# Twelve scalings by a third, made by GpSimd instead of VectorE, in a gated dilated convolution

## The chip, the core and the metric

The kernel runs on one core of a Trainium2 chip. A core has TensorE (matrix products, "PE" in the profile), VectorE ("DVE"), ScalarE ("ACT"), GpSimd ("POOL") and SyncE ("SP", which issues transfers here), each with its own queue of instructions, worked off in order. SBUF is the on-chip memory; PSUM holds what TensorE sums up. The metric is the device time of one execution in microseconds (us).

## The reference

The input x has 2 sequences of 16000 steps with 256 channels, in bf16. A causal convolution with three taps, two steps apart, makes 512 channels; the first 256 go through tanh, the others through a sigmoid; their product is multiplied by a 256x256 matrix.

```python
dil = 2
pad = (K - 1) * dil                      # K = 3
h = xp[t + 4] @ w[0] + xp[t + 2] @ w[1] + xp[t] @ w[2]   # xp: x with pad zeros ahead
f, g = h[..., :256], h[..., 256:]
z = tanh(f) * sigmoid(g)
out = z @ w_o
```

## The kernel before, in words

**Groups.** The time axis is cut into groups. One short group (kind P) at the start is computed tap by tap. The others save matrix products by the algebra of fast convolutions. A group of kind B takes four neighbouring steps a row, two pairs of outputs, and needs four products instead of six. A group of kind A takes six steps a row, three pairs of outputs, and needs five products instead of nine. There are 13 A groups (numbered 0 to 12) of 256 rows. What the products multiply are not the inputs but sums of them, each a tile of 128 partitions by 1024 bf16 elements (two steps of the pair, two halves of the channels, 256 rows). For an A group `operand` (L325) names them:

- u0, u1, u2, e: differences, and f: a sum, of two views of the input tile xt;
- u3 = u1 / 3, uh = -u1 / 2, ud = 2 u1: the scalings;
- rm = e + u3, rp = f + u1, r0 = u0 + uh, ri = u2 + ud: these replace e, f, u0 and u2 in place (`ON_TOP`, L362), and TensorE multiplies them. It also multiplies u1 itself. So in the profile TensorE reads them under the names e, f and u.

**Who makes them.** `pre` (L365) issues one of these operations on the engine that it is given, for all four quarters of 256 elements or for a slice of them. VectorE makes the differences and the scalings. GpSimd makes ri, quarter by quarter, and part of the operands m, p, d0 and d3 of the B groups. rm, rp and r0 are made by transfers that add while they land (L377), issued from GpSimd's queue. So u3 has one reader: the transfer that adds it onto e. The tiles of u3 rotate through two buffers (`sum_pool`), those of e, f and u through three.

**After the products.** TensorE sums the products into PSUM banks. ScalarE copies the first one to SBUF (ss, L432). VectorE combines (L435): a, and for A groups also hh and yy, each 128x512 fp32 from one SBUF and one PSUM operand. ScalarE applies tanh and sigmoid (L475), VectorE multiplies the two (the gate, zz, L494, two SBUF operands in bf16), TensorE multiplies by w_o (L512), ScalarE moves the result to SBUF (L537) and SyncE stores it.

**What sets the order.** The order of all queues is written out by hand in `PLAN` (L13), one line for each of the blocks, with four fields: TensorE, ScalarE, VectorE, GpSimd. A block is one group and one of four tiles of 128 output channels. Tokens of the third field are VectorE's instructions in order: a, y, h (the combinations), g (a gate product), v, and names such as `u3.4`, which means u3 of A group 4. Tokens of the fourth field are GpSimd's, and are issued where the third field has its `a`. A token of the fourth field that computes is held (`hold`, L353): it waits for the VectorE instruction that was issued last, or one before it for every apostrophe (`made_v`, `gpsimd`, L569). The call gives the reason: "GpSimd reads SBUF while VectorE's sums read PSUM". Such a line is

```python
 F Z P L I | a y c b e e | g u0.4 u3.4 f.4 a y | r0.3 ri.3 m.6''
```

Here VectorE makes a gate product, u0, u3 and f of group 4, then a and y; GpSimd issues the transfer r0 of group 3, a quarter of ri of group 3 and a quarter of m of B group 6.

The loop over the lines dispatches the tokens of the third field one by one; what is none of the letters goes to `sums` (L565), which calls `pre` with VectorE and notes the instruction for later holds.

Of the kernel before, what the change touches and what calls it, by code (L numbers as in the profile page):

```python
# [123 lines left out]
def kernel(  # L124
# [10 lines left out]
    nc = tc.nc  # L135
# [189 lines left out]
    def operand(g, name):  # L325

        G = groups[g]
        R = G["R"]
        prev, cur = views(g)
        v = lambda n: G[n][:, :, :, :R]  # L330
        if G["kind"] == "B":
            return {
                "m": lambda: (ALU.subtract, None, cur[0], prev[1]),
                "p": lambda: (ALU.add, None, cur[0], prev[1]),
                "d0": lambda: (ALU.subtract, None, prev[0], cur[0]),
                "d3": lambda: (ALU.subtract, None, cur[1], prev[1]),
            }[name]()
        return {
            "u0": lambda: (ALU.subtract, None, prev[1], cur[0]),
            "u1": lambda: (ALU.subtract, None, prev[2], cur[1]),  # L340
            "u2": lambda: (ALU.subtract, None, cur[2], cur[0]),
            "e": lambda: (ALU.subtract, None, cur[0], prev[2]),
            "f": lambda: (ALU.add, None, cur[0], prev[2]),
            "rp": lambda: (ALU.add, None, v("f"), v("u1")),
            "u3": lambda: (None, 1.0 / 3.0, v("u1"), None),
            "rm": lambda: (ALU.add, None, v("e"), v("u3")),
            "uh": lambda: (None, -0.5, v("u1"), None),
            "ud": lambda: (None, 2.0, v("u1"), None),
            "r0": lambda: (ALU.add, None, v("u0"), v("uh")),
            "ri": lambda: (ALU.add, None, v("u2"), v("ud")),  # L350
        }[name]()

    def hold(ins, behind):  # L353
        if behind is not None:
            tc.add_manual_dep(
                ins.ins, behind.ins.name,
                mybir.DependencyInfo(mybir.DependencyClass.Sync, mybir.DependencyReason.DATA),
                reason="GpSimd reads SBUF while VectorE's sums read PSUM",
            )
        return ins  # L360
# [4 lines left out]
    def pre(g, name, eng, qs=slice(0, 4), behind=None):  # L365
        G = groups[g]
        R = G["R"]
        op, factor, a, b = operand(g, name)
        if name not in G:
            if name in ON_TOP:  # L370

                G[name] = G[ON_TOP[name]]
            else:
                pool = {"m": pre_pool, "p": pre_pool, "u3": sum_pool, "uh": sum_pool, "ud": sum_pool, "d0": dif_pool, "d3": dif_pool}.get(name, dif_pool)
                G[name] = pool.tile([P, 2, CT, RG], bf16, name=name, tag=name)
        if name in BY_DMA:
            return nc.gpsimd.dma_start(out=G[name][:, :, :, :R], in_=b, accum_op=op)  # L377
        o, a, b = (t if t is None else t.rearrange("p q ct r -> p (q ct) r")[:, qs] for t in (G[name][:, :, :, :R], a, b))
        if op is None:
            ins = eng.tensor_scalar_mul(o, a, factor)  # L380
        else:
            ins = eng.tensor_tensor(out=o, in0=a, in1=b, op=op)  # L382
        return hold(ins, behind)
# [43 lines left out]
    def copy_first(blk):  # L427
        g, oi = blk
        G = groups[g]
        n = 2 * G["R"]  # L430
        G["ss", oi] = ss_pool.tile([P, 2 * RG], f32, name="ss")
        nc.scalar.copy(out=G["ss", oi][:, :n], in_=G["b", oi][:, :n])  # L432
# [84 lines left out]
    def out_evict(g, rb0, jp, on_v=False):  # L517
        G = groups[g]
        J = G["J"]
        o_ps = G["o", rb0, jp]  # L520
        copy = (lambda **a: note(nc.vector.tensor_copy(**a))) if on_v else nc.scalar.copy  # L521
        t0 = G["t0"] + J * rb0
        if jp is None:
            odd = osb_pool.tile([P, D], bf16, name="odd", tag="odd")
            copy(out=odd[:], in_=o_ps[:, 0, :])
            n = G["R"] - rb0
            assert J * n == P
            store = dict(out=out[G["b"], t0:t0 + J * n, :].rearrange("(r q) d -> q r d", q=J), in_=odd[:])
            if g == seq[-1][0]:
                last_odd.append(store)  # L530
            else:
                nc.sync.dma_start(**store)
            return
        if ("osb", rb0) not in G:
            G["osb", rb0] = osb_pool.tile([P, J, D], bf16, name="osb", tag=f"osb{J}")
        osb = G["osb", rb0]
        copy(out=osb[:, 2 * jp:2 * jp + 2, :], in_=o_ps[:])  # L537
        G["out", rb0] = G.get(("out", rb0), 0) + 1
        if G["out", rb0] == J // 2:
            nc.sync.dma_start(  # L540
                out=out[G["b"], t0:t0 + J * P, :].rearrange("(p j) d -> p j d", j=J), in_=osb[:]
            )
# [14 lines left out]
    def note(ins):  # L557
        made_v.append(ins)
        return ins

    def group_of(token):
        name, n = token.split(".")
        return (Bs if name in ("m", "p", "d0", "d3") else As)[int(n)], name

    def sums(tokens):  # L565
        for token in tokens:
            note(pre(*group_of(token), nc.vector))
# [54 lines left out]
    for k, line in enumerate(PLAN.strip().split("\n"), -1):  # L622
        pe, act, dve, pool = (part.split() for part in line.split("|"))
        b0, b1, b2, b3 = (seq[n] if 0 <= n < N else None for n in (k, k - 1, k - 2, k - 3))
        if ">" in dve:
            sums(dve[:dve.index(">")])
            dve = dve[dve.index(">") + 1:]
        waiting, done = list(act), set()

        def scalar():  # L630

            while waiting:
                what = waiting[0]
                there = {"c": "F" in done, "b": "Z" in done, "e": made, "E": made[1:], "d": not leftover}
                if not there.get(what, True):
                    break
                waiting.pop(0)
                if what == "c":
                    copy_first(b0)
                elif what in "by":  # L640
                    activate(b2, what)
                elif what == "a":
                    activate(b3, "a")
                elif what == "d":
                    activate((0, 3), "a")
                elif what == "w":
                    weights_a(1 + K)
                else:
                    out_evict(*made.pop("eE".index(what)))

        scalar()
        for what in pe:
            if what in "FM":
                product(b0, {"F": "first", "M": "mid"}[what])
            elif what == "L":
                product(b1, "last")
            elif what in "ZI":
                product(b2, {"Z": "zero", "I": "inf"}[what])
            elif what == "D":
                direct(3, (leftover.pop(0),), (1,))  # L660
            elif what == "H":
                piece, (bank, tag) = next(firsts)
                out_mm(*piece, dts=(0,), pool=bank, tag=tag)
            elif what == "R":
                made.append(next(seconds))
                out_mm(*made[-1], dts=(1,))
            else:
                made.append(todo.pop(0))
                out_mm(*made[-1], **({"pool": ps_b, "tag": "b"} if what == "p" else {}))
            done.add(what)  # L670
            scalar()
        assert not waiting, (k, waiting)

        for what in dve:
            if what == "g":
                gate(b3[0], b3[1] // 2)
                if b3[1] == 3 and b3 != seq[-1]:
                    todo += pieces_of(b3[0])
            elif what == "G":
                gate(0, int(k > 0))  # L680
                if k > 0:
                    todo += pieces_of(0)
            elif what == "a":
                gpsimd(pool)
                combine(b1, "a")
            elif what == "y":
                combine(b1, "y")
            elif what == "h":
                halfway(b0)
            elif what == "v":  # L690
                out_evict(*made.pop(0), on_v=True)
            else:
                sums((what,))

        while loaded < len(loads) and wanted[loads[loaded]] <= k + LOAD:
            load(loads[loaded])
            loaded += 1
# [34 lines left out]
```

## Time and profile before

| what | value |
| --- | --- |
| time, two runs | 263.03 and 263.12 us, median 263.07 |
| span of the profiled execution, first to last instruction | 261.4 us |
| the profiled execution's time outside the span, by the runs' median | 1.7 us |
| granted TensorE clock | 0.999 |
| VectorE's instructions that scale a 128x1024 tile (u3, uh, ud) | 3 x 13 |

The profile is of one execution. Its lines give an engine, a line of the kernel, the operation, the tiles as out<-in with the buffer numbers left out, and the shape. In the timelines the first two columns are the start, counted from the span's start, and the duration, in us; x2 at the end means two instructions merged, and brackets give the idle time ahead and what ended it. In the groups' rows the numbers behind the bar are the busy time in us and the mean duration in ns. Because u3 is a tile of the name u with a number, it stands in the profile as u; the scaling by a third is the row "TENSOR_SCALAR u<-u" of L380. On GpSimd, "u<-u,ud" is a quarter of ri.

### The profile page before, as it was taken

The page shows a single profiled execution, that of the slowest core. Times are in us where ns is not written, and L with a number is a line of the kernel's source. Part 1 is how long each engine was busy: PE and PEld are TensorE (multiplying, and loading weights), DVE is VectorE, ACT ScalarE, POOL GpSimd, SP SyncE. Part 2 cuts the span into 40 slices and gives each one's busy share as a digit, 9 for nine tenths or more (in the row PEclk, how much of TensorE's full clock was granted, in tenths as well). Part 3 has the DMA queues.
Part 4 walks back from the last instruction along what each step waited for, and adds up shares of the span by engine and source line. Part 5 has one row for each costly group of instructions (what it writes and reads, how often), then busy time and mean ns, then how long its engine had stood idle before and what let it go on. Part 6 is the DMA issues. An engine that isn't in the chain of part 4 may idle for free.

```text
span 261.4 us, 4534 instructions
## 1 busy us (share of the span) xinstructions
PE 256.5 (98%) x1484; PEld 144.2 (55%) x1484; DVE 240.5 (92%) x401; ACT 243.7 (93%) x492; POOL 136.2 (52%) x204
## 2 busy tenths in 40 slices
PE   8999999999999999999999999999999999999993
PEld 5654565545545555555555555555555555665682
DVE  2899999999999999999999999999999999977773
ACT  4989998999999999999999999999999999999993
POOL 1033355687765577956757685643746453431100
PEclk9999999999999999999999999999999999999999
DMA  6999979999969667969895799959825574462115
GB/s 185 215 168 212 262 177 174 227 211 179 212 152 232 139 147 143 228 147 230 197 197 135 175 214 190 239 160 201 237 41 127 149 152 116 129 160 109 76 61 210
DMA packets 81663, 45.20 MB, mean 173 GB/s; under 512 B 68936, under 2 KB 70216, under 8 KB 81640
## 3 DMA queue, kind: packets, MB, share of 16 engines
q1 hardware_dynamic: 75112, 33.74, 54.6%
q0 software_dynamic: 5616, 10.23, 23.2%
q10 hardware_dynamic: 912, 0.95, 1.1%
q8 instruction: 11, 0.18, 0.3%
q14 instruction: 12, 0.10, 0.1%
HBM read 1.25 MB, written 16.38 MB: 67 GB/s over the span
## 4 chain that ended last, share of the span: by engine, by line
PE 97%; DMA 1%; DVE 0%; issue 0%
PE b L401 57%; PE o_ps L512 21%; PE a L401 16%; PE b L421 1%; PE a L421 1%; DMA xn<-in_x_dram 1%; PE tp L308 0%; DVE osb L521 0%; PE fill L248 0%
## 5 line engine op out<-in xcount | busy, mean ns | idle before, releaser
L435 DVE SCALAR_TENSOR_TENSOR a<-ss,b 128x512 f32<-128x512 f32 (+2 forms) x100 | 67.1, 672 | 7.9 <-ACT sg L475 3.1
L537 ACT CAST osb<-o_ps 128x512 bf16<-128x512 f32 x119 | 69.8, 622 | 0.8 <-PE o_ps L512 0.7
L512 PE MATMUL o_ps<-wo_sb,zz 128*128 128x256 bf16 x496 | 70.5, 273 | 0.0
L432 ACT COPY ss<-b 128x512 f32<-128x512 f32 (+2 forms) x100 | 59.6, 597 | 4.6 <-PE b L401 3.5
L512 PEld LDWEIGHTS <-zz 128*128 128x128 bf16 x496 | 48.4, 98 | 25.2 <-DVE zz L494 0.2
L401 PEld LDWEIGHTS <-w_sb 128*128 128x128 bf16 x400 | 39.0, 98 | 36.8 <-issue 0.2
L382 POOL TENSOR_TENSOR u<-u,ud 128x256 bf16<-128x256 bf16 x52 | 39.8, 772 | 24.9 <-DVE zz L494 9.1
L382 POOL TENSOR_TENSOR d<-xt 128x256 bf16<-128x256 bf16 (+2 forms) x56 | 33.4, 606 | 32.7 <-DVE zz L494 13.0
L494 DVE TENSOR_TENSOR zz<-th,sg 128x1536 bf16<-128x1536 bf16 (+2 forms) x52 | 40.9, 788 | 0.5 <-ACT sg L475 0.2
L435 DVE SCALAR_TENSOR_TENSOR yy<-hh,b 128x512 f32<-128x512 f32 x52 | 35.4, 680 | 1.9 <-PE b L401 1.8
L435 DVE SCALAR_TENSOR_TENSOR hh<-ss,b 128x512 f32<-128x512 f32 x52 | 35.4, 681 | 1.2 <-PE o_ps L512 0.5
L475 ACT ACTIVATE sg<-b 128x512 bf16<-128x512 f32 (+2 forms) x50 | 30.5, 610 | 2.1 <-PE b L401 1.4
L475 ACT ACTIVATE th<-b 128x512 bf16<-128x512 f32 (+2 forms) x50 | 30.5, 610 | 1.9 <-PE b L401 1.6
L475 ACT ACTIVATE sg<-a 128x512 bf16<-128x512 f32 (+2 forms) x50 | 31.0, 619 | 0.0
L401 PE MATMUL b<-f,wp_sb 128*128 128x512 bf16 x104 | 30.9, 379 | 0.0
L401 PE MATMUL b<-u,w_sb 128*128 128x512 bf16 x104 | 30.9, 379 | 0.0
L401 PE MATMUL a<-u,w_sb 128*128 128x512 bf16 x104 | 30.9, 379 | 0.0
L401 PE MATMUL b<-u,wa_sb 128*128 128x512 bf16 x104 | 30.9, 379 | 0.0
L401 PE MATMUL b<-e,wm_sb 128*128 128x512 bf16 x104 | 30.9, 378 | 0.0
L475 ACT ACTIVATE th<-a 128x512 bf16<-128x512 f32 (+2 forms) x50 | 30.5, 614 | 0.3 <-PE a L401 0.2
L401 PEld LDWEIGHTS <-wp_sb 128*128 128x128 bf16 x200 | 19.5, 98 | 20.1 <-issue 0.7
L401 PEld LDWEIGHTS <-wm_sb 128*128 128x128 bf16 x200 | 19.5, 98 | 17.0 <-issue 0.4
(59 smaller groups left out, 342.7 us busy)
## 6 DMA issues: line engine op xcount, KB each, us to landing
out_dram<-osb SPq DMA_DIRECT2D x26, 384.0 KB, 2.6
out_dram<-osb SPq DMA_DIRECT2D x23, 256.0 KB, 3.0
f<-u POOLq DMA_DIRECT2D x13, 256.0 KB, 3.5
e<-u POOLq DMA_DIRECT2D x13, 256.0 KB, 4.4
u<-uh POOLq DMA_DIRECT2D x13, 256.0 KB, 5.3
w_sb<-in_w_dram ACTq DMA_DIRECT2D x3, 256.0 KB, 4.1
xt<-in_x_dram SPq DMA_TRANSPOSE x25, 7.2
xn<-in_x_dram SPq DMA_DIRECT2D x1, 160.0 KB, 3.2
```

The costliest lines, as they stand in the source:

```text
L382: ins = eng.tensor_tensor(out=o, in0=a, in1=b, op=op)
L401: nc.tensor.matmul(G[bank, oi][:, :2 * R], lhsT=wmat[:, ct, osl], rhs=G[mv][:, :, ct, :R], start=which == "first" and ct == 0, stop=ct == ...
L421: nc.tensor.matmul(G[bank, oi][:, :4 * r].rearrange("p (j r) -> p j r", j=4), lhsT=w_taps[tap][:, ct, osl], rhs=xt[:, j0:j0 + 4, ct, c0 + ...
L432: nc.scalar.copy(out=G["ss", oi][:, :n], in_=G["b", oi][:, :n])
L435: return note(nc.vector.scalar_tensor_tensor(out=out, in0=in0, scalar=scalar, in1=in1, op0=ALU.mult, op1=op))
L475: nc.scalar.activation(out=G[name, dt][:, j:j + 2, :R], in_=G[bank, oi][:, :2 * R].rearrange("p (q r) -> p q r", q=2), func=(ACT.Tanh, ACT ...
L494: note(nc.vector.tensor_tensor(out=G["z"][:, dt, :, :n], in0=G["th", dt][:, :, :n], in1=G["sg", dt][:, :, :n], op=ALU.mult))
L512: nc.tensor.matmul(o_ps[:, q, :], lhsT=z, rhs=wo_sb[:, dt, :], start=dt == 0 and (q == 0 or len(dts) == NT), stop=dt == NT - 1, skip_group ...
L537: copy(out=osb[:, 2 * jp:2 * jp + 2, :], in_=o_ps[:])
```

## The change

In the loop over VectorE's tokens a case is added ahead of the last one: a token u3.n with n over 0 is issued on GpSimd, in two halves of two quarters each where n is odd, in one instruction where n is even.

```diff
             elif what == "v":
                 out_evict(*made.pop(0), on_v=True)
+            elif what.startswith("u3") and int(what[3:]):
+                n = int(what[3:]) % 2 + 1
+                for q in range(0, 4, 4 // n):
+                    pre(*group_of(what), nc.gpsimd, slice(q, q + 4 // n))
             else:
                 sums((what,))
```

`pre` is called without a VectorE instruction to be held behind, and the new instructions are not noted in `made_v`, so that an apostrophe in the fourth field counts VectorE's remaining instructions. The place in the program is the token's: on GpSimd the scaling comes after what earlier lines and tokens gave it, and ahead of the fourth field's tokens of its line where u3 stands before `a`. Twelve scalings (groups 1 to 12) become 18 instructions on GpSimd: two of 128x512 for the odd groups, one of 128x1024 for the even ones. The scaling of group 0 stays on VectorE. TensorE's, ScalarE's and SyncE's instructions stay as they are.

## The prediction

> **What bounds the kernel now.** I read the engine shares first, then the chain that ended last, then TensorE's waits, then five stretches of 40 us through the steady part (their sum is quoted), and last the timelines of VectorE (DVE) and GpSimd (POOL) side by side.
>
> ```profile
> span 261.4 us, 4534 instructions
> PE 256.5 (98%) x1484; PEld 144.2 (55%) x1484; DVE 240.5 (92%) x401; ACT 243.7 (93%) x492; POOL 136.2 (52%) x204
> PE 97%; DMA 1%; DVE 0%; issue 0%
> PE a L216 <- PEq L716: 0.8, 1, 0.8
> sum 200.00, PE 200.00 PEld 109.64 DVE 193.26 ACT 192.82 POOL 123.07; mean PE 40.00 PEld 21.93 DVE 38.65 ACT 38.56 POOL 24.61
> ```
>
> TensorE is the bound: 97% of the chain, one wait of 0.8 us at the very start (the only one that the list of waits has for it), and 200.00 busy us of the 200 between 40 and 240 us. Work taken off VectorE cannot shorten that. VectorE is busy 193.26 of the same 200 us, so it has 3% in hand and becomes the bound soon when something delays it; GpSimd, with 123.07, has room. So the question is not what the moved work saves but whether, in its new place, it makes VectorE late and TensorE behind it.
>
> **What is removed.** Twelve scalings of 128x1024 leave VectorE's queue (the thirteenth, of group 0, stays).
>
> ```profile
> L380 DVE TENSOR_SCALAR u<-u 128x1024 bf16<-128x1024 bf16 x13 | 5.5, 423 | 0.0
> 50.48 0.67 POOL L382 TENSOR_TENSOR u<-u,ud 128x256 bf16<-128x256 bf16 x1
> 51.18 0.42 DVE L380 TENSOR_SCALAR u<-u 128x1024 bf16<-128x1024 bf16 x1
> 51.52 0.69 DVE L382 TENSOR_TENSOR e<-xt 128x1024 bf16<-128x1024 bf16 x1
> 52.41 0.70 DVE L435 SCALAR_TENSOR_TENSOR a<-ss,b 128x512 f32<-128x512 f32 x1 [0.21 <-PE b L401]
> ```
>
> One is 0.42 us long, and its successor starts 0.34 us behind it (51.18 to 51.52; I use 0.33). VectorE is spared 12 x 0.33 = 4.0 us. Since TensorE has nothing to gain, I count a third of a microsecond at each place only against a delay at the same place.
>
> **What is added: the length.** GpSimd gets six scalings of 128x1024 and twelve of 128x512, 18 instructions. The trace has no such instruction on GpSimd. The nearest rows:
>
> ```profile
> masks.py:199 POOL TENSOR_SCALAR_AFFINE_SELECT ident<-ident 128x128 bf16<-128x128 bf16 x1 | 0.3, 292 | 0.1
> L382 POOL TENSOR_TENSOR d<-xt x56: 398/606/1123, 49.3 to 247.7; 128x256 bf16<-128x256 bf16 x40, 128x160 bf16<-128x160 bf16 x8, 128x128 bf16<-128x128 bf16 x8
> L382 POOL TENSOR_TENSOR u<-u,ud x52: 658/667/1125, 33.1 to 236.4; 128x256 bf16<-128x256 bf16 x52
> L382 DVE TENSOR_TENSOR u<-xt x39: 673/685/1215, 21.7 to 227.8; 128x1024 bf16<-128x1024 bf16 x39
> ```
>
> (Numbers after the count: shortest, median, longest in ns.) The two-input sum of GpSimd takes 398 ns at 128 elements (its shortest) and 606 at 256 (its median): 208/128 = 1.6 ns an element on top of 190 ns. The one-input row, the select of 128 elements, has 292 - 190 = 102 ns left: 0.8 ns an element. A one-input scaling at that rate is 190 + 1024 x 0.8 = 1.01 us, a half 0.60. At the rate of the slower sum, (667 - 190)/256 = 1.86 ns, it is 2.1 and 1.14 us. The lower end follows from the nearest row in kind, one input; I take a little over it, **1.1 us whole and 0.65 us for a half**, and keep 1.0 and 2.1 as ends. The Trainium skill, GPSIMD Engine Reference, section 4.1 Engine selection, calls one-input work "roughly line-rate"; by that and the 1.2 GHz of its section 1, an estimate of 0.85 us whole, and a sum below of about +1.2 us. Section 3.1 of that page of the Trainium skill has 2.6 cycles an element for a two-input sum, an estimate of 2.2 us whole, and a sum above +12 us. The select's row lies nearer to the first.
>
> **What is added: the collision.** GpSimd's load is no limit: 6 x 1.1 + 12 x 0.65 = 14.4 us on 123 of 200. What matters is that VectorE's sums and GpSimd's sums do not run together:
>
> ```profile
> 82.92 1.29 POOL L382 TENSOR_TENSOR u<-u,ud 128x256 bf16<-128x256 bf16 x2
> 83.55 1.22 DVE L382 TENSOR_TENSOR u<-xt 128x1024 bf16<-128x1024 bf16 x1
> 37.92 0.69 DVE L382 TENSOR_TENSOR u<-xt 128x1024 bf16<-128x1024 bf16 x1
> 38.09 1.04 POOL L382 TENSOR_TENSOR u<-u,ud 128x256 bf16<-128x256 bf16 x1 [1.10 <-DVE zz L494]
> ```
>
> In the first pair GpSimd's second sum ends at 84.21, 0.66 us after VectorE's began; VectorE took 1.22 instead of 0.69, 0.53 more. In the second pair VectorE ends 0.52 us after GpSimd's start, and GpSimd takes 0.38 more than 0.66. So the later one waits, until 0.13 us before the end of the other. The Trainium skill, SBUF — State Buffer, section Who interferes with whom, says that a VectorE instruction with two SBUF inputs contends with a GpSimd one that reads SBUF and that the loser waits for the whole instruction; the trace agrees but for those 0.13 us, which over the ten holds below would add 1.3 us. The four-field lists avoid the collision: a sum in GpSimd's list is held behind a named VectorE instruction, so that it runs beside sums that read PSUM. The moved scalings have no such hold and start when their predecessor on GpSimd ends. That place is in the timelines:
>
> ```profile
> 39.08 0.87 POOL L377 DMA_DIRECT2D u<-uh  x1
> 40.04 0.68 DVE L494 TENSOR_TENSOR zz<-th,sg 128x1024 bf16<-128x1024 bf16 x1
> 68.74 1.12 POOL L382 TENSOR_TENSOR u<-u,ud 128x256 bf16<-128x256 bf16 x1
> 69.86 0.94 DVE L494 TENSOR_TENSOR zz<-th,sg 128x1536 bf16<-128x1536 bf16 x1
> 86.93 0.61 POOL L382 TENSOR_TENSOR d<-xt 128x256 bf16<-128x256 bf16 x1
> 87.94 0.68 DVE L494 TENSOR_TENSOR zz<-th,sg 128x1024 bf16<-128x1024 bf16 x1
> 125.09 0.66 POOL L382 TENSOR_TENSOR u<-u,ud 128x256 bf16<-128x256 bf16 x1
> 125.96 0.69 DVE L382 TENSOR_TENSOR u<-xt 128x1024 bf16<-128x1024 bf16 x1
> 131.81 1.52 POOL L382 TENSOR_TENSOR m<-xt 128x256 bf16<-128x256 bf16 x2 [0.89 <-DVE u L382]
> 133.40 1.55 DVE L494 TENSOR_TENSOR zz<-th,sg 128x1024 bf16<-128x1024 bf16 x2
> 151.58 0.90 POOL L382 TENSOR_TENSOR u<-u,ud 128x256 bf16<-128x256 bf16 x1
> 152.80 0.69 DVE L382 TENSOR_TENSOR f<-xt 128x1024 bf16<-128x1024 bf16 x1
> 193.92 0.85 POOL L382 TENSOR_TENSOR d<-xt 128x160 bf16<-128x160 bf16 x2
> 194.94 0.69 DVE L382 TENSOR_TENSOR u<-xt 128x1024 bf16<-128x1024 bf16 x1
> 214.37 0.44 POOL L382 TENSOR_TENSOR d<-xt 128x160 bf16<-128x160 bf16 x1
> 215.09 0.69 DVE L382 TENSOR_TENSOR u<-xt 128x1024 bf16<-128x1024 bf16 x1
> ```
>
> Each pair: the instruction ahead of the scaling on GpSimd, and the VectorE instruction that it meets. The hold is the scaling's start + its length - 0.13 - VectorE's start.
>
> - Group 2 (whole; rows at 50.48 to 52.41): start 51.15; with the scaling gone VectorE comes to its sum at 51.18 and is held to 52.12, 0.60 later than the 51.52 of before; 0.21 of it was a wait for TensorE anyway: 0.4.
> - Group 8 (whole): start 152.48; the sum at 152.80 begins at 153.45: 0.65.
> - Group 6 (whole): 125.75; held 0.76, less 0.33: 0.43. Group 10: 194.77; held 0.80, less 0.33: 0.47. Group 4: 87.54; held 0.57, less 0.33: 0.24.
> - Group 7 (halves): the first from 133.33 holds the gate product 0.45 us; the second starts behind it and holds the next one 0.47: 0.92 less 0.33, 0.59. Group 1 likewise from 39.95: 0.43 and 0.47, less 0.33: 0.57. Group 3 from 69.86: 0.52 by the first half, none by the second, less 0.33: 0.19.
> - Groups 5, 9, 11 and 12: the scaling meets sums that read PSUM, or a sum for less than 0.33 us. The last pair is group 12: VectorE's sum, drawn forward to 214.76, is ahead of the scaling's 214.81. Nothing.
>
> Sum: 0.4 + 0.65 + 0.43 + 0.47 + 0.24 + 0.59 + 0.57 + 0.19 = **3.5 us**. A delay passes to TensorE, as VectorE frees its PSUM buffers; what the buffers swallow (unknown, up to some 0.3 us a place) I set against what GpSimd's sums behind a scaling, out of step with their holds, cost in further collisions.
>
> **What is moved.** GpSimd's transfers stand behind the scalings, above all the one that adds the third onto e, which TensorE reads.
>
> ```profile
> 196.95 0.88 POOL L377 DMA_DIRECT2D e<-u  x1 [2.17 <-DVE u L380]
> 203.22 0.59 PE L401 MATMUL b<-e,wm_sb 128*128 128x512 bf16 x2
> DMA to landing us min/median/max: 3.3/4.4/9.1
> ```
>
> Here, in group 10, the issue waited for VectorE's scaling; now the scaling ends at 194.77 + 1.1 and it is issued earlier. Issue to use is 6.3 us against a median landing of 4.4, so about 1.9 us are free. Elsewhere a transfer moves back by 1.1 to 2 us. I cost it at nothing; without that cover it would be up to 1 us a group.
>
> The profiled execution has a span of 261.4; the runs' median of 263.07 has 1.7 us around it. Span 264.9, time 263.1 + 3.5 = **266.6 us**, 1.3% slower; 2% is about what a measurement of this kernel can tell from no change, so this is within it.
>
> **The rivals.**
>
> - *GpSimd scales more slowly than it reads.* From 1.3 us whole and 0.75 half on, the five whole collisions cost 0.2 more each, the five half ones 0.1, the near misses (5, 9, 12) begin to hold: past +5.3 us, over the 2%. At 2.1 and 1.14 us: five x 1.0, five x 0.5, and some 1.5 for the others on top of 3.5, 275.6 us. For it: no row shows a multiplication on GpSimd, and the spread between its own sums (606 and 667) shows that the body matters. Against: the select. The 2.6 cycles of the Trainium skill's GPSIMD Engine Reference, section 3.1, would belong here. Chance 0.37; about 270 in the middle.
> - *No collision: not slower.* GpSimd reads one input, and if that leaves VectorE's second input free, or if GpSimd reaches its scalings after VectorE's sums have begun (four starts above are within 0.1 us of each other), VectorE keeps the 4.0 us and TensorE stays full: 263.1 us, no gain. It decides where the mean hold is under 0.33 us. Against: the holds in the trace come with reads of SBUF on both sides. Chance 0.11.
> - *The third comes late to TensorE.* If a scaling and its transfer are behind by over 1.9 us, TensorE waits for e, up to 1 us in each of twelve groups: 268 to 275. Chance 0.03.
>
> That the change does not do what it says is no rival: the order of the built program has twelve scalings fewer on VectorE and the 18 on GpSimd, TensorE's and ScalarE's unchanged.
>
> **How the numbers follow.** Forecast 0.49, slow scaling 0.37, no collision 0.11, late third 0.03. The forecast's own range is 264.8 to 268.3 (lengths of 1.0 to 1.3 us, buffers swallowing half). The whole range goes to 264.0 below, leaving out the no-collision case, and to 273 above, leaving out the slowest quarter of the slow scalings. Faster by over 2%: TensorE is full, 0.01. Within: 0.49 + 0.11, 0.60. Slower: 0.39.
>
> **What would show it.** A row of POOL TENSOR_SCALAR at about 1.1 us for 128x1024 and 0.65 for 128x512; VectorE's two-input sums (e, f, u, zz) with a longest of 1.5 us and more, TensorE's waits showing VectorE's a, hh and yy as releasers; VectorE's busy time up by some 2 us although it has twelve instructions fewer. Wrong, if the scalings take over 1.3 us, if VectorE's longest sums stay at 1.2 us, or if TensorE waits for e.

## The result, and the profile after

The changed kernel takes 276.48 us (276.26 to 276.70) against 263.07: a ratio of 1.0499, 95% interval [1.0476, 1.0521], 13.4 us slower. The forecast was 266.6, the range ended at 273.0: the time lies above it, on the side of the first rival.

The page of the kernel after, its span, its engines' shares, and the chain that ended last:

```profile
span 274.9 us, 4542 instructions
PE 261.4 (95%) x1484; PEld 144.4 (53%) x1484; DVE 253.9 (92%) x389; ACT 245.1 (89%) x492; POOL 175.6 (64%) x222
PE 66%; DVE 17%; ACT 8%; DMA 4%; issue 4%; POOL 0%; ACTq 0%; DVEq 0%
```

The sum over the five stretches from 40 to 240 us, then TensorE's waits (total us, times, longest):

```profile
sum 200.00, PE 191.52 PEld 102.01 DVE 195.33 ACT 180.58 POOL 157.04; mean PE 38.30 PEld 20.40 DVE 39.07 ACT 36.12 POOL 31.41
...
PE b L401 <- DVE hh L435: 3.1, 3, 1.7
PE a L401 <- DVE a L435: 1.3, 2, 0.9
PE b L401 <- DMA e<-u: 1.3, 1, 1.3
PE b L401 <- DVE a L435: 0.9, 3, 0.5
PE a L401 <- POOL d L382: 0.9, 1, 0.9
PE a L216 <- PEq L720: 0.8, 1, 0.8
PE b L401 <- DVE yy L435: 0.6, 2, 0.4
```

TensorE is no longer full: 191.52 of 200, and its share of the chain is 66% where it was 97%. Without the 0.8 us at the start, which the kernel before has too, the waits listed are 8.1 us in few and long pieces, mostly for VectorE's combinations hh, a and yy. Its own busy time is 4.9 us longer too (261.4 against 256.5) for the same 1484 products. Together 13.0 of the 13.5 us by which the span has grown. VectorE, with twelve instructions fewer, is busy 2.1 us more in the 200 us.

The groups of the new instructions on GpSimd (busy us, mean ns, idle before), and two kinds of VectorE's own instructions (shortest, median, longest ns):

```profile
L380 POOL TENSOR_SCALAR u<-u 128x512 bf16<-128x512 bf16 x12 | 18.9, 1608 | 0.0
L380 POOL TENSOR_SCALAR u<-u 128x1024 bf16<-128x1024 bf16 x6 | 17.1, 2851 | 0.0
L382 DVE TENSOR_TENSOR u<-xt x39: 676/689/2835, 21.6 to 241.4; 128x1024 bf16<-128x1024 bf16 x39
L380 DVE TENSOR_SCALAR ud<-u x13: 413/420/3272, 30.0 to 234.7; 128x1024 bf16<-128x1024 bf16 x13
```

A scaling takes 2.85 and 1.61 us in the mean, not 1.1 and 0.65: 36.0 us of GpSimd's time instead of the 14.4 worked out. VectorE's longest wait made one of its own scalings (ud, 0.42 us) last 3.27. In the kernel before, the longest of these took 0.57 (the row below), and the longest of its u sums 1.22, not 2.84:

```profile
L380 DVE TENSOR_SCALAR ud<-u x13: 416/418/572, 30.2 to 221.1; 128x1024 bf16<-128x1024 bf16 x13
```

One such place, VectorE's and GpSimd's timelines of the kernel after:

```profile
143.26 3.27 DVE L380 TENSOR_SCALAR ud<-u 128x1024 bf16<-128x1024 bf16 x1
139.51 3.37 POOL L380 TENSOR_SCALAR u<-u 128x512 bf16<-128x512 bf16 x2
142.83 0.89 POOL L377 DMA_DIRECT2D u<-uh  x1
143.48 0.96 POOL L382 TENSOR_TENSOR u<-u,ud 128x256 bf16<-128x256 bf16 x1
144.11 0.89 POOL L382 TENSOR_TENSOR d<-xt 128x256 bf16<-128x256 bf16 x1
144.68 0.94 POOL L382 TENSOR_TENSOR p<-xt 128x256 bf16<-128x256 bf16 x1
145.30 0.93 POOL L382 TENSOR_TENSOR u<-u,ud 128x256 bf16<-128x256 bf16 x1
```

The two halves of u3.7 end at 142.88. VectorE's long wait comes behind them, not beside them: a transfer and four sums of GpSimd follow without a pause until 146.23, and VectorE's scaling is done only then, at 146.53. By the list two of these sums were held behind instructions that VectorE had done while the halves ran, the other two behind its sum e, which ends at 143.34: each was free to start before the one ahead of it had ended. Neighbouring sums there overlap: 143.48 + 0.96 is 144.44, and the next starts at 144.11.

### The profile page after: what moved, and what is told of

It reads as the page before. It is cut to its first block, busy times and chain, and to the rows that moved or that the text cites. A ratio compares the mean times of both kernels' runs of the same rounds, so it can differ in the third digit from the quotient of the medians.

```text
span 274.9 us, 4542 instructions
## 1 busy us (share of the span) xinstructions
PE 261.4 (95%) x1484; PEld 144.4 (53%) x1484; DVE 253.9 (92%) x389; ACT 245.1 (89%) x492; POOL 175.6 (64%) x222
## 4 chain that ended last, share of the span: by engine, by line
PE 66%; DVE 17%; ACT 8%; DMA 4%; issue 4%; POOL 0%; ACTq 0%; DVEq 0%
PE b L401 38%; PE o_ps L512 14%; PE a L401 10%; DVE a L435 4%; DVE zz L494 4%; DMA e<-u 4%; DVE hh L435 3%; ACT osb L537 2%; ACT th L475 2%; ACT ss L432 2%; DVE yy L435 2%; ACT sg L475 1%; PE b L421 1%; PE a L421 1%; PE a L216 1%
## 5 line engine op out<-in xcount | busy, mean ns | idle before, releaser
L382 POOL TENSOR_TENSOR u<-u,ud 128x256 bf16<-128x256 bf16 x52 | 44.1, 867 | 17.6 <-DVE zz L494 5.9
L382 POOL TENSOR_TENSOR d<-xt 128x256 bf16<-128x256 bf16 (+2 forms) x56 | 36.8, 677 | 28.2 <-DVE zz L494 11.6
L494 DVE TENSOR_TENSOR zz<-th,sg 128x1536 bf16<-128x1536 bf16 (+2 forms) x52 | 45.8, 882 | 0.2 <-ACT sg L475 0.2
L380 POOL TENSOR_SCALAR u<-u 128x512 bf16<-128x512 bf16 (+1 forms) x18 | 36.0, 2022 | 0.0
L382 DVE TENSOR_TENSOR u<-xt 128x1024 bf16<-128x1024 bf16 x39 | 31.5, 814 | 0.0
```

The costliest lines, as they stand in the source:

```text
L494: note(nc.vector.tensor_tensor(out=G["z"][:, dt, :, :n], in0=G["th", dt][:, :, :n], in1=G["sg", dt][:, :, :n], op=ALU.mult))
```

## The experiments

Two theories stood at first. *Direct hold*: a scaling keeps VectorE's sums out while it lasts. *Lateness*: a long instruction on GpSimd makes its later sums come in a bunch, and these keep VectorE out, or TensorE waiting. Times against the kernel before in the same runs (median 263.06 to 263.26):

| edit | time, us | ratio [95%] |
| --- | --- | --- |
| third made on no engine | 263.12 | 0.9999 [0.9985, 1.0014] |
| only even groups moved (wholes) | 268.68 | 1.0205 [1.0182, 1.0228] |
| only odd groups moved (halves) | 270.60 | 1.0282 [1.0261, 1.0303] |
| copy in place of the scaling | 267.22 | 1.0153 [1.0134, 1.0172] |
| one short fill in its place | 265.07 | 1.0069 [1.0051, 1.0087] |
| fills as long as the scaling | 280.97 | 1.0682 [1.0638, 1.0727] |
| a product of two tiles in its place | 279.49 | 1.0613 [1.0598, 1.0628] |
| halves held behind VectorE | 287.13 | 1.0909 [1.0885, 1.0933] |
| after, a small fill ahead of each sum | 282.80 | 1.0736 [1.0679, 1.0794] |
| after, without the ri sums | 271.83 | 1.0326 [1.0309, 1.0343] |
| before, without the ri sums | 263.86 | 1.0020 [1.0007, 1.0032] |
| after, GpSimd's sums in turn | 277.03 | 1.0527 [1.0508, 1.0546] |
| before, GpSimd's sums in turn | 265.06 | 1.0063 [1.0044, 1.0083] |

**How long a scaling is.** Behind the kernel before, GpSimd makes single instructions with no other work beside them.

```diff
+    for n in (128, 256, 512, 1024):
+        nc.gpsimd.tensor_scalar_mul(t_out[:, 0:n], t_in[:, 0:n], 1.0 / 3.0)
...
+    nc.gpsimd.tensor_copy(out=t_out[:], in_=t_in)
+    nc.gpsimd.tensor_tensor(out=t_out[:], in0=t_in, in1=t_in, op=ALU.add)
```

> The kernel before, with seven test instructions at the end of GpSimd's queue, where nothing waits for them: scalings by a third of 128, 256, 512 and 1024 bf16 elements, one of 512 fp32 elements, a copy and a two-input sum of 1024. If the scaling itself is slow on GpSimd, the bf16 ones take 0.25 + 2.4 ns an element also here: 0.86 us for 256, 1.48 for 512, 2.76 for 1024. If they were slow in the changed kernel because VectorE was beside them, they take 0.4, 0.6 and 1.0 us here. The prediction's rule for two inputs (0.19 us + 1.6 to 1.86 ns an element) gives 1.8 to 2.1 us for the sum; the copy, with one input and no arithmetic, tells whether it is the multiplication (1.0 us) or the one-input form (2.7 us).

The tests' rows, L705 the four scalings in bf16 (shortest and longest are 128 and 1024 elements), L707 the copy, L708 the sum of two:

```profile
L705 POOL TENSOR_SCALAR t_out<-w_sb x4: 544/1168/2769, 249.0 to 252.1; 128x128 bf16<-128x128 bf16 x1, 128x256 bf16<-128x256 bf16 x1, 128x512 bf16<-128x512 bf16 x1, 128x1024 bf16<-128x1024 bf16 x1
L707 POOL COPY t_out<-w_sb 128x1024 bf16<-128x1024 bf16 x1 | 1.0, 1038 | 0.0
L708 POOL TENSOR_TENSOR t_out<-w_sb 128x1024 bf16<-128x1024 bf16 x1 | 1.9, 1891 | 0.1
```

2.77 us whole: (2769 - 544)/896 = 2.5 ns an element, 2.7 times a copy and 1.5 times a sum with two inputs. The number of inputs does not set the time; the length read off the select belonged to another instruction. The Trainium skill, GPSIMD Engine Reference, section 4.1 Engine selection, calls one-input work "roughly line-rate"; the copy may pass for that, the scaling does not.

**What VectorE's freed time is worth.** The third is made nowhere; rm adds group 0's third for every group, so that the output isn't that of the reference.

```diff
-            "rm": lambda: (ALU.add, None, v("e"), v("u3")),
+            "rm": lambda: (ALU.add, None, v("e"), None),
...
+        if name == "rm":
+            b = third[:, :, :, :R]
...
-            else:
+            elif not what.startswith("u3") or what == "u3.0":
                 sums((what,))
```

> The scalings of groups 1 to 12 are left out altogether: the transfer adds the third of group 0 in every group, so the result is not the reference's. This is the value of the 12 x 0.33 us that VectorE is spared. TensorE was the bound: 263.1 us, at most 0.3 less. A rival is that VectorE's lateness cost TensorE something all along: then up to 1 us less.

Nothing, to 0.15%: that step of the prediction holds, and all of the 13.4 us comes from what was added.

**Which half of the change.** Only the even groups' thirds move, then only the odd groups'.

```diff
-            elif what.startswith("u3") and int(what[3:]):
+            elif what.startswith("u3") and int(what[3:]) and int(what[3:]) % 2 == 0:
```
```diff
-            elif what.startswith("u3") and int(what[3:]):
+            elif what.startswith("u3") and int(what[3:]) % 2:
```

> Only the six even groups, in one instruction each, go to GpSimd (17.1 of the 36 us that GpSimd takes for all); the odd ones stay on VectorE. Direct hold: by the prediction's list 0.4 + 0.65 + 0.43 + 0.47 + 0.24 = 2.2 us, 265.3. Occupancy: about half of the 13.4 us of the change, 269 to 270; less than half if the delays of neighbouring groups build on each other, 266 to 268.

> Only the six odd groups, in two halves each, go to GpSimd. If the costs of the groups simply add, 13.4 us of the change less 5.5 of the even groups: 271. If delays of neighbouring groups build on each other, less: 267 to 269.5. The prediction's list of direct holds has 0.57 + 0.19 + 0.59 = 1.35 us for them: 264.5.

5.5 and 7.5 us, 13.0 together: the cost is made group by group, about 1.1 us a group. The groups in two halves cost no less than the wholes; since they stand at other places, this does not tell what the cutting itself does.

**What GpSimd does in the place of the scaling.** Four kernels with the instruction exchanged at the same 18 places: a copy (the factor is left out), one fill that reads nothing, fills as long as the scalings (u3 is then a constant in both), and a product with a tile of thirds.

```diff
-            ins = eng.tensor_scalar_mul(o, a, factor)
+            if name == "u3" and eng is nc.gpsimd:
+                ins = eng.tensor_copy(out=o, in_=a)
+            else:
+                ins = eng.tensor_scalar_mul(o, a, factor)
```
```diff
...
+                for h in ((0, 1), (1, 2)) if int(what[3:]) % 2 else ((0, 2),):
+                    nc.gpsimd.memset(u3[:, slice(*h)], 1.0)
```
```diff
...
+                for n in ((2, 1, 2, 1) if int(what[3:]) % 2 else (2, 2, 2)):
+                    nc.gpsimd.memset(u3[:, 0:n], 1.0)
```
```diff
-            ins = eng.tensor_scalar_mul(o, a, factor)
+            if name == "u3" and eng is nc.gpsimd:
+                ins = eng.tensor_tensor(out=o, in0=a, in1=third[:, qs], op=ALU.mult)
+            else:
+                ins = eng.tensor_scalar_mul(o, a, factor)
```

> As the changed kernel, but GpSimd copies u1 instead of scaling it (the factor is left out, the result is not the reference's). A copy of 1024 takes 1.04 us and one of 512 about 0.55, close to the 1.1 and 0.65 that the prediction took for the scaling. So this is the case of the prediction's sum: 266.6, its own range 264.8 to 268.3. Outside of it, the sum was wrong in more than the length.

> In the scalings' places GpSimd fills the third's tile with a constant once, 0.95 us for a whole and 0.53 for a half: as short as the copy, but without reading (VectorE's scalings are left out as in the change, the result is not the reference's). If the copy's 4.1 us are VectorE's waits for what GpSimd reads: 263.1 to 264. If they are GpSimd's lateness: 266 to 267.5, as with the copy.

> In the scalings' places GpSimd fills the third's tile with a constant, three fills of 512 x 2 elements for a whole (3 x 0.95 us) and fills of 1024 and 512 for each half (0.95 + 0.53 us): GpSimd is taken as long as in the changed kernel but reads nothing, so VectorE's sums need not wait for the scaling itself. VectorE's twelve scalings are left out as in the change; the result is not the reference's. Theory occupancy: what is left of the 13.4 us without the 3.5 of direct holds, 271 to 274. Theory direct hold: 263 to 264.

> As the changed kernel, but GpSimd makes the third by multiplying u1 with a tile that holds a third (two inputs) instead of by a constant: 1.8 to 2.1 us for 1024 elements, 1.0 to 1.15 for 512, less than the 2.76 and 1.48 of the changed kernel, but with VectorE's sums held for nearly the whole of it, not for 0.9 us. Theory occupancy (what costs is how long GpSimd is taken, which puts its other sums out of step): faster than the changed kernel, 269 to 273 us. Theory direct hold (what costs is VectorE's sum that meets the scaling): holds of 1.7 to 1.9 us instead of 0.8, slower than the changed kernel, 280 us or more.

Added to the time of before:

| | reads SBUF | only writes |
| --- | --- | --- |
| about 1 us a group (copy 1.04; fill 0.95) | +4.1 | +1.8 |
| about 2.8 us a group (scaling 2.77; fills 2.9) | +13.4 | +17.9 |

With the length that the prediction assumed, its time comes out: 267.2 against 266.6. Of those 4.1 us, 1.8 are there without any read, so by difference about 2.3 go with the reads, as direct holds would. At the true length the reads are not needed at all for a loss of this size, so direct hold falls as the main cause: length does it. That fills cost even more than scalings, and more than either theory expected, is left open; what can be seen is that VectorE isn't held beside them and is held the longer behind them. From the timelines with the long fills:

```profile
76.42 3.12 DVE L382 TENSOR_TENSOR f<-xt 128x1024 bf16<-128x1024 bf16 x1
73.12 3.13 POOL L696 MEMSET u<- 128x1024 bf16 x4
76.20 0.88 POOL L377 DMA_DIRECT2D f<-u  x1
76.81 1.59 POOL L382 TENSOR_TENSOR p<-xt 128x256 bf16<-128x256 bf16 x2
78.07 0.90 POOL L382 TENSOR_TENSOR d<-xt 128x256 bf16<-128x256 bf16 x1
```

VectorE's sum, asked for 0.17 us after the last fill has ended, takes 3.12 instead of 0.69: it waits for a transfer and three of GpSimd's own sums.

The two-input product is shorter than the scaling (2208 ns a whole, in the row below) and yet dearer. Its 279.5 us is near what direct hold had forecast (280 or more) and not what lateness had (269 to 273), so an instruction that holds VectorE for nearly its whole length pays for that too:

```profile
L384 POOL TENSOR_TENSOR u<-u,third 128x1024 bf16<-128x1024 bf16 x6 | 13.2, 2208 | 0.0
```

**How long a scaling holds.** Why the scaling is cheaper than the product shows in the kernel after itself, around a whole scaling (u3 of group 4):

```profile
91.00 1.00 DVE L494 TENSOR_TENSOR zz<-th,sg 128x1024 bf16<-128x1024 bf16 x1
91.93 0.68 DVE L382 TENSOR_TENSOR u<-xt 128x1024 bf16<-128x1024 bf16 x1
90.42 2.77 POOL L380 TENSOR_SCALAR u<-u 128x1024 bf16<-128x1024 bf16 x1
```

The gate product takes 1.00 instead of 0.68: it gets in at 91.32, 0.90 us after the scaling's start, and the next sum runs at full speed while the scaling goes on to 93.19. So a 2.77 us scaling held VectorE for 0.9 us only. The wholes that start at 51.89 and 131.56 let a sum of VectorE in after 0.89 us each. The prediction's rule (until 0.13 us before the end) is that of sums with two inputs; by it a scaling of 2.77 us would have cost some 1.7 us at each whole more than one of 1.1.

**Where the backlog comes in.** If lateness is the cause, placing each half where VectorE reads PSUM should help (24 halves, each held behind VectorE's last instruction ahead of an a). If VectorE merely needs a gap, a fill of 64 elements between GpSimd's sums gives one. And if GpSimd's total load is the measure, leaving out the 52 sums of ri (TensorE then multiplies u2 in its place) takes it back to that of before.

```diff
...
+                    pre(*group_of(w), nc.gpsimd, slice(q, q + 2), behind=made_v[-1])
                 gpsimd(pool)
...
+            elif what.startswith("u3") and int(what[3:]):
+                halves += [(what, 0), (what, 2)]
```
```diff
+            nc.gpsimd.memset(gap[:], 0.0)
             pre(g, name, nc.gpsimd, slice(had, quarters[g, name]), behind=behind)
```
```diff
+            if name == "ri":
+                G = groups[g]
+                G["ri"] = G["u2"]
+                continue
```

> All twelve scalings on GpSimd in halves (24 x 1.49 us = 36 us, as in the change), each put ahead of the fourth field's tokens at an a of the third field and held behind the VectorE instruction before that a, so that its first 0.5 us run beside a sum that reads PSUM. Theory direct hold: the cost is gone, 263 to 265. Theory occupancy: GpSimd is taken as long as before and its own sums come late: 268 to 273, a few us under the changed kernel.

> As the changed kernel, with a short fill of 64 elements (about 0.15 us, reads nothing, needed by nobody) ahead of every quarter sum that GpSimd makes by its fourth field. Theory runs (what costs is that late GpSimd sums follow each other without a pause, so that VectorE's sum waits for three to five of them): VectorE gets in at the pauses, its longest two-input sums fall from 2.8 us to about 1.5, and the time falls to 269 to 273 although GpSimd has some 10 us more to do. Theory occupancy alone (GpSimd is late, its sums and transfers are late for TensorE): slower than the changed kernel, 278 to 281.

> As the changed kernel, with GpSimd's 52 quarter sums for ri left out (34 us of its work; TensorE multiplies u2 instead, the result is not the reference's). GpSimd then has as much to do as in the kernel before. Theory occupancy and runs: the late work catches up quickly, what is left is VectorE's wait for the scalings' own reading, the 4.1 us of the copy or less: 264.5 to 267.5. Theory length (a long scaling costs by itself, however much else GpSimd has): 274 to 277.

> The kernel before without the 52 quarter sums for ri, for comparison with the run without them in the changed kernel (the result is not the reference's). TensorE is the bound: 263.1, at most 0.3 less.

Held halves are the worst of all, +24 us, where both theories had expected less than the change costs; so this run decides nothing between them: the list's order makes each wait in GpSimd's queue, 27.9 us idle ahead of them, and everything behind them with it. The row, then the page of the kernel after without ri:

```profile
L380 POOL TENSOR_SCALAR u<-u 128x512 bf16<-128x512 bf16 x24 | 36.9, 1540 | 27.9 <-DVE zz L494 8.2 <-DVE uh L380 5.9 <-DVE f L382 4.0
```
```profile
PE 257.8 (95%) x1484; PEld 144.4 (53%) x1484; DVE 248.3 (92%) x389; ACT 244.2 (90%) x492; POOL 133.5 (49%) x170
```

Small fills make it dearer by 6.3 us, at a granted clock of 0.98 to 0.99, and open no gap: VectorE's longest u sum lasts 3.36 us there. Without ri GpSimd is busy 133.5 us, less than the 136.2 of before, and the kernel still loses 8.6 us (the same cut in the kernel before: 0.6). So the total load alone is not the measure, though some 5 of the 13.4 us go with the ri sums: the 271.8 us lies between the two expectations. What is left is the long instruction at its place, with sums due behind it.

**Why VectorE waits through several sums.** First the rule by itself, behind the kernel before: a VectorE read of PSUM releases GpSimd's instructions, VectorE reads PSUM once more and then asks for a two-input sum of 128x1024 (0.69 us free).

```diff
...
+    tests = [lambda n=n: [add(k) for k in range(n)] for n in (1, 2, 3, 5)]
+    tests += [lambda: [add(0) for _ in range(4)]]
+    tests += [lambda: [f for k in range(4) for f in (add(k), fill(k))]]
+    tests += [lambda: [third(k) for k in range(4)]]
+    tests += [lambda: [nc.gpsimd.tensor_scalar_mul(t_o[:, 0:1024], t_w[0], 1.0 / 3.0)]]
...
```

> Tests at the end of the kernel before. A VectorE read of PSUM (128x512) releases GpSimd's instructions; VectorE then reads PSUM once more (about 0.55 us) and comes to a two-input sum of 128x1024 (0.69 us when free), so that this sum is asked for about 0.5 us after GpSimd began. GpSimd has 1, 2, 3, 5 sums of 128x256 (0.66 us each) back to back; then 4 that write the same place; 4 with a fill of 64 elements behind each; 4 scalings of 256; one scaling of 1024. Theory that VectorE is not let in between instructions that follow one another on GpSimd: the sum takes 0.69, then about 1.4, 2.0 and 3.3 us, growing by 0.66 with each GpSimd sum; with fills between as with 4 sums or more, 2.7 to 3.5 us. Rival, turn by turn: VectorE comes in at the end of the GpSimd sum that is under way, at most 0.6 us late, so 0.7 to 1.3 us for every number of sums. One scaling of 1024, which lasts 2.77 us: 0.7 to 1.1 us if it holds VectorE only in its first 0.9 us, 2.9 if it holds to its end.

The theory fell as it was put: 0.69, 1.16, 1.16, 1.16 us for 1, 2, 3, 5 sums. VectorE and GpSimd take turns. It took 0.69 us behind four sums to one place, four sums with fills between them and four scalings of 256; with the scaling of 1024 it took 0.91, let in 0.89 us after that had begun. But the traces show how the places of the long waits differ: they lie behind a transfer's issue on GpSimd's queue, and there the sums overlap by 0.3 us. So the tests were made again with a transfer ahead.

```diff
...
+    tests = [lambda n=n: [move()] + [add(k) for k in range(n)] for n in (1, 2, 3, 5)]
+    tests += [lambda: [move()] + list(in_turn(5))]
+    tests += [lambda: [move(), nc.gpsimd.tensor_scalar_mul(t_o[:, 0:1024], t_w[0], 1.0 / 3.0)]]
...
```

> The tests of the last run again, with a transfer of GpSimd's queue (the kind that adds while it lands, 128x1024) issued directly ahead of the sums, so that VectorE's two-input sum is asked for at about the start of the first of 1, 2, 3, 5 GpSimd sums. New theory: behind a transfer's issue each GpSimd instruction starts about 0.3 us before its predecessor ends (the traces of the changed kernel have it so), and VectorE's sum doesn't get in between them: 0.69 + about 0.6, 1.2, 1.8, 3.0 us, growing by 0.6 with each GpSimd sum. Rival: as without the transfer, at most 1.2 us for every number. With the five sums made to wait each for its predecessor, by the theory at most 1.8 us (the overlap can hold for the first only); with one scaling of 1024 behind the transfer the theory says 2.8 to 3.4 us, the rival 0.9 to 1.2.

VectorE's sum and GpSimd's five, first without a transfer:

```profile
282.81 1.16 DVE L722 TENSOR_TENSOR t_s<-w_sb 128x1024 bf16<-128x1024 bf16 x1
282.13 3.61 POOL L706 TENSOR_TENSOR t_o<-w_sb 128x256 bf16<-128x256 bf16 x5 [0.81 <-DVE t_s L716]
```

Then behind one, and behind one with each sum made to wait for the one before it:

```profile
286.47 4.14 DVE L729 TENSOR_TENSOR t_s<-w_sb 128x1024 bf16<-128x1024 bf16 x1
286.01 0.87 POOL L709 DMA_DIRECT2D wm_sb<-w_sb  x1 [5.28 <-DVE t_s L707]
286.62 3.43 POOL L706 TENSOR_TENSOR t_o<-w_sb 128x256 bf16<-128x256 bf16 x5
...
295.79 1.67 DVE L729 TENSOR_TENSOR t_s<-w_sb 128x1024 bf16<-128x1024 bf16 x1
295.33 0.88 POOL L709 DMA_DIRECT2D w_sb<-w_sb  x1 [5.28 <-DVE t_s L707]
295.93 4.29 POOL L706 TENSOR_TENSOR t_o<-w_sb 128x256 bf16<-128x256 bf16 x5
```

Behind a transfer the wait does grow: 1.92, 2.29, 2.90, 4.14 us for 1, 2, 3, 5 sums, 0.62 a sum from the second on, and VectorE ends some 0.56 us after the last one. The waits are 0.4 to 0.6 us longer than expected; VectorE's sum begins while the transfer is still being issued, 0.14 to 0.40 us ahead of the first GpSimd sum. Where each sum waits for its predecessor VectorE is let in after the first. One scaling of 1024 behind a transfer held VectorE's sum to 2.05 us, between the two expectations: VectorE is let in 1.2 us after the scaling's start, early here too. What each part of GpSimd does meanwhile, no trace shows. The Trainium skill would explain it: Perfetto Trace Analysis, DMA Instruction — SWDGE (GPSIMD), says that two of GpSimd's eight cores prepare such a transfer, and GPSIMD Engine Reference, section 2.1 Instruction dispatch, that a core starts the next instruction as soon as its own share is done. Six cores would then run ahead of two, and SBUF would never be free for VectorE between two sums; the overlap of 0.3 us agrees.

**Is that lock-out the price?** The kernel after, and the kernel before as control, with each sum of GpSimd also waiting for the computing instruction before it on GpSimd (the last hunk is for the kernel after alone).

```diff
...
-            pre(g, name, nc.gpsimd, slice(had, quarters[g, name]), behind=behind)
+            ins = pre(g, name, nc.gpsimd, slice(had, quarters[g, name]), behind=behind)
+            if made_g:
+                hold(ins, made_g[-1])
+            made_g.append(ins)
...
-                    pre(*group_of(what), nc.gpsimd, slice(q, q + 4 // n))
+                    made_g.append(pre(*group_of(what), nc.gpsimd, slice(q, q + 4 // n)))
```

> The changed kernel, but each sum of GpSimd also waits for the computing instruction before it on GpSimd, which is no new order but leaves a pause of about 0.08 us between two of them. Theory (behind a transfer's issue GpSimd's sums overlap and shut VectorE out): the pauses end the overlap, VectorE comes in after one sum, its longest waits fall from 2.6 and 2.8 us to under 1.5, and the time falls from 276.5 to 267 to 272. Rival (the scalings' length and GpSimd's backlog alone): the pauses lengthen the backlog by 100 times 0.08 us, so 276 or more.

> Control: the kernel before with the same additional waits between GpSimd's sums. Both theories: 263 to 265 us, since GpSimd mostly pauses there for VectorE anyway.

The long lock-outs go, the loss stays. VectorE's operand sums, and TensorE's waits, of the kernel after in turn:

```profile
L382 DVE TENSOR_TENSOR u<-xt x39: 675/687/1935, 22.1 to 241.9; 128x1024 bf16<-128x1024 bf16 x39
...
PE a L401 <- POOL d L382: 2.5, 2, 1.4
PE a L401 <- POOL u L382: 2.0, 2, 1.1
PE a L401 <- DVE a L435: 1.6, 3, 0.8
PE b L401 <- DVE hh L435: 1.2, 2, 0.8
```

The longest of these sums falls from 2.84 to 1.94 us (not to the 1.5 expected), TensorE's waits for hh from 3.1 to 1.2. In their place TensorE waits 4.5 us for GpSimd's own sums d and u, and the time is 277.0. The control pays 2.0 us for its pauses, some 0.5 of it outside the span from first to last instruction. If they cost as much in the kernel after, an estimate of 1.0 to 1.4 us of the 13.4 is the lock-out's own (2.0 - 0.55, less those 0.5 at the lower end). It decides who is late, VectorE or GpSimd. What makes somebody late is that 2.8 to 3.2 us of scaling a group stand ahead of sums which TensorE needs soon.

## Why the prediction was wrong, point by point

- *TensorE is the bound, VectorE's freed 4.0 us are worth nothing*: right, 263.12 us without the third.
- *The length, 1.1 and 0.65 us, ends 1.0 and 2.1*: the step that failed first. Measured 2.77 and 1.49 undisturbed, above even the upper end, and over the 1.3 us that the prediction gave as a sign of being wrong. The rate was taken from the select because it has one input; a copy has one input too and would have fitted (1.04). The step mis-sized GpSimd's added time by 36.0 against 14.4 us.
- *The collisions, 3.5 us in all*: fair in size for the assumed length. The copy costs 4.1, of which about 2.3 go with its reads; that the total still fits the forecast is partly luck, since 1.8 us of lateness, which the sum had at nothing, fill the gap. The rule itself doesn't hold for a scaling of 1024, which lets VectorE in after 0.9 us.
- *Sums out of step set off against what the PSUM buffers swallow*: the step that failed second, and the larger one. At about 1 us a group it is 1.8 us, at 2.8 us a group 17.9, both with instructions that read nothing.
- *The moved transfers at nothing*: nearly right. TensorE waited for e behind a transfer once, 1.3 us.
- *The first rival, slow scaling*: the case that came. Its 275.6 us for 2.1 us scalings lies near the measured time by another mechanism: it let every hold grow with the length, while the holds stayed near 0.9 us and lateness grew. Being near is luck: carried on to the lengths measured, its rule gives 3.5 + 5 x 1.67 + 5 x 0.84 + 1.5 = 17.6 us, some 281.
- *1.3% counted as no more than a measurement can tell*: the intervals here reach 0.6% to either side at most, most of them 0.2%, so 3.5 us would have been a clear change.
- *What would show it*: VectorE's busy time did rise by 2.1 us, and hh, a and yy are TensorE's releasers; the longest sums, 2.84 us against "1.5 and more", said that a run of instructions and not one was waited for.

Not settled: why fills of the same length cost 4.5 us more than the scalings, and how the 13.4 us divide between VectorE's and GpSimd's lateness, since each takes the other's place.

## What to carry to other kernels

Look for the very operation, on that engine, in a trace before sizing a move to GpSimd; where there is none, a kind of instruction and a count of inputs don't stand in for it, and the range has to reach past the dearest row. Ask first which sums are due behind the moved instruction and how soon TensorE needs them: an engine that is idle nearly 40% of the time still has no room of 2.8 us at a given place. Making the holds tidier only passes the delay on.

## What the runs showed of the hardware

- GpSimd scales at 2.5 ns an element, 128 partitions wide, in bf16; 512 elements took 1.49 us in fp32 as well. A copy of 1024 takes 1.04, a two-input sum 1.89.
- Such a scaling keeps VectorE's sum with two SBUF inputs out for only its first 0.9 us of 2.77.
- Behind a transfer issued by GpSimd, its sums overlap by 0.3 us and VectorE isn't let in until they pause: 4.14 us for a sum of 0.69 behind five of them, against 1.16 without the transfer.
- In one place of the kernel after, TensorE's granted clock falls behind two pauses. Three stretches of the kernel after (busy us of each engine, then the clock), and products before and in the middle one:

```profile
140.00:146.00 6.00, 4.50 (x25) 2.11 (x22) 6.00 (x6) 4.93 (x10) 6.00 (x7) 1.00 1.13 142
146.00:151.50 5.50, 4.76 (x18) 2.19 (x19) 4.42 (x8) 2.74 (x6) 2.58 (x4) 0.69 0.67 144
151.50:157.00 5.50, 5.50 (x33) 3.00 (x31) 4.89 (x9) 4.72 (x10) 4.03 (x5) 1.00 0.35 99
...
146.72 0.60 PE L401 MATMUL b<-e,wm_sb 128*128 128x512 bf16 x2 [1.29 <-DMA e<-u]
148.58 1.06 PE L401 MATMUL a<-u,w_sb 128*128 128x512 bf16 x2
```

After waits of 0.93 and 1.29 us the clock is 0.69 over 5.5 us, and two products take 1.06 us instead of 0.60. That is an estimate of 5.5 x 0.31 = 1.7 us. It is no rule here: with halves held TensorE waited up to 1.80 us at a time, in turn up to 1.4, both at a mean clock of 1.00. Nor does the clock explain the 4.9 us by which TensorE is busy longer: in turn it is busy 261.3 us as well. Records of neighbouring products overlap (two take 0.59 us, one alone 0.38), so pauses between products lengthen the busy time although no product is longer; how much of the 4.9 us that is, is open.
